# One filter's spectrum by dense products instead of two stages, fewer filler products, and a newly searched order

## The chip, the core and the metric

The kernel runs on one core of a Trainium2 chip. The core has a matrix engine (TensorE, "PE" in the profile, with its weight loads as "PEld"), a vector engine (DVE), an activation engine (ACT), a small general engine (POOL) and a queue engine (SP) that issues transfers to 16 DMA engines. Time is device microseconds for one launch, as a median of several runs. A profiled execution is a separate run with a trace; its span is counted from its first instruction to its last.

## What is computed

The input has one sequence of 2048 positions and 640 channels. Two layers follow each other, each with a residual:

```python
x = A_q
h  = x + q_ln * y            # q_ln = layernorm(x)
k_shift = short causal filter of k (4 taps per channel)
kv = k_shift * v
y  = causal convolution of kv with ssm_k (length 2048, per channel, by FFT) + kv * ssm_D
h2 = h + (silu(n @ w_gate) * (n @ w_up)) @ w_down     # n = layernorm(h), inner width 1728
```

## The kernel before

**Tiling.** The sequence is cut into 4 blocks (j = 0 to 3) of 512 positions, the channels into two column halves (c = 0, 1) of 320. For each block and half, the spectra of `kv` (called X) and of the filter `ssm_k` (called K) are formed on PE, multiplied with those of the earlier blocks on DVE, summed, and transformed back on PE. Then come the first residual (ACT and DVE), the layer norm (DVE, ACT, POOL), a transpose of the normalized block, and the feed-forward part: gate and up products into PSUM, SiLU on ACT, a product on DVE, and the down projection.

**Two ways to a spectrum.** `fwd` (line 659) and `spec` (line 741) do it in two stages. Stage one, named `s1`, is 4 groups of 2 matmuls (128x128 weights by 320 columns), each group evicted from PSUM by ACT (`e1`). Then four transfers within SBUF (`shK…`, `shX…`, 160 KB each) regroup the partitions. Stage two, named `s2`, is 4 groups of 4 matmuls with 128x64 weights, each group evicted by ACT (`e2`). `dense_h` (line 689) does it in one stage: 4 groups (`df`) of 8 matmuls of 128x128 weights by 320 columns, each group evicted by ACT or DVE (`de`), with no transfer between. Its tables (`DEN`, line 462) lie where the down-projection weights come later, so the loads `wd` wait for every dense group (line 701 collects them). Block 0 uses the dense way throughout. In block 1 the set `DFW` (line 351) names what goes the dense way: before, the filter K of the first half alone.

**Guard matmuls.** `warm` (line 542) makes matmuls of 512 columns on constants whose result nobody reads. `WARM` (line 339) asks for one run of 5 at the start and one run of 4; `FILL` (line 340) asks for four runs of 2. The order decides where they stand. In the order of before, the run of 5 and one run of 2 stand at the start, ahead of the first tap products, and the run of 4 and three runs of 2 stand among the work between the end of block 0's convolution and the start of its feed-forward part.

**The order.** No engine chooses at run time. A packed table (`_PLAN`, line 1327) holds, for each of the operations, its engine, its place in that engine's queue, its buffer, and some pacing of transfers; `plan` (line 101) unpacks it, and `emit` writes five instruction streams with the semaphore waits that the dependences need. Each engine runs its stream strictly in order. In the order of before, the two-stage spectrum of K of block 1's second half (`K11`) stands as follows on PE: three groups of `s1K11` together after the dense groups of `K10`, the fourth a little later between two guard runs, and the four groups of `s2K11` spread among block 0's gate and up products. On SP its four transfers `shK11` stand among the loads of the feed-forward weights; the last of them stands behind three weight loads.

Of the kernel before, what the change touches and what calls it, by code (L numbers as in the profile page):

```python
# [317 lines left out]
def bass_sequential_preLN__ssm_conv_h3__swiglu_ffn__prompt_kernel(  # L318
# [3 lines left out]
    _, S, D = A_q.shape  # L322
    F = B_w_gate.shape[1]
    assert (S, D, F) == (2048, 640, 1728)
    R = 4
    B = 128 * R
    NB = S // B
    N = 2 * B
# [10 lines left out]
    WARM = [5, 4]  # L339
    FILL = [2] * 4  # L340
# [10 lines left out]
    DFW = {("K",1,0)}  # L351
# [976 lines left out]
    "c-rlI2UJ^Ew)Q#dsGtfGl0XOv6%b7ziUdMPfT#k|d$GZkxWv78C+=~axc7n++i{C~Z*g3bICdP{vEv%Ixc8E{zKvoW%w*<eX3bkO|N3+9y1MtCv(Mh&{`PmSE{h`qA|it8z^<K$nl}O*xYg0J5fSN6?)ddiXm!;b"  # L1328
    "h49+{ZxPzY!LM5hZ!G`p-EY@_`}v=VNO+Si;jK}`*LKZqq(8m4-SF!?{(X19U6We%5?aOmN7w(l4q7wW`uIKT-)qyhPHo5jtM-I9iXi-r_5X(JzXk8_oMIQ>q`%Yp|EGHXQI$x4m-j#7|L^tvdp!MLDe=EO$3LT9"
    "!e8qBC!R6?{8Q#X|6KgP!rYp3((B`oTL1PNmhf-5ZmX=8NWVw?=UWJ_cQit)H<{*4n%~RFhytHPWPsKf6o+D6{S=o46WSTb4Qxn=ji`u+=!lD0NPsv<gOXj>bm;Lyo`{cxNDQqcmrp99!R`irny=|_#RN|r<PJV~"  # L1330
    "a7BZWTo@@v9?-@Fk3u9uQaA*#`yd(eMSe&EUOkW!`6Ct5x>`dasxOL1R_KjHMkGh!C=vWqz#rRX?FR7}fJg%VIbf><8wKDKp+FRZf{-3sgwU@;!6*zxfNwuIVjyo5GD8#v#EL@+$bxKO6N1uE28^<!RIpD$>3|>;"
    "<)AF&Km{ltvMWJls2s+|p=^|gicle7sX$fW&kTDIc=v#jdhpcDtp(Z=z;iZu$^Z{JfIc2oqZ(*UhTbHX4<~p@Lb+%l^jaad4fbTz4Mt_4cBliyu0$UInl#ji8UR^4^f7uDbw(Z0J8)l*=Acr*Pz_eaa5WlrMSW2("
    "u<eGLpnWzPf!;@>(0H^HbwWeY7&H#NZHLhl(1&OenvC|ME@%K6jE2G34d9ao%z6T&-cT<o)XNLlQ~+x-s7WYr+>Fu!84QA$Rgg;|_@F{n-Jt?J7^!fLlOZ*D@PR9DsEG>dpoU!w9ECx~xlqYy6a_Uch8)^M7IhH0"
    "8F?Mt)dKEZunGaIW;SafuXxyvz)mOB9q_)3dI08rfVl=L(jID(30!sqAM>DZKJ@fPi@|b%D-StD4uE)ih!_gmZ&pGyRIwR@70!WBdljfT0Ir%pW8kcXb1JZ&3AO8k`hx~CU{oX;0!;M;@59l1Xe6-O6A*QRDis3{"
    "<)9G<j2H@xmqBGC!P6*Ud<1Yl7JcO6yE`!71FBa9S{ev-`V>4Y0<Znha>#xuT7o`<_WtN|sKYwQuO7VBp_OR0EAmEA{1))n01+C|3b1YNnTHml+h`ipdNEv0K(o+A@Y{qogY9&%c>)#-p#Hl-IiI5!P~|nCfG;4{"
    "T13Dz!G1oP3##}CodGPnKoQfx>nret@sH>ybO~KSN<0sJhmN9S=mZkrS?DA>h0daL$QRE=U!iZ%A@l?C#B*S_MF78%z_Jn8)&U=7pxE}HluF378=3+fd<crU01;OK%9ZFj%xDAHCb?!tXQ+Jhd`W}(;sic(T*|jY"
    "Z!uK33Ro*~&7>^o%L3lZfuUMZL>*wB4m#-#*L^@qpP-q*?i92P;;aW&HUV4PAh#({kEu|N?qIVD7}^S4>_$7#m*{IW5h^+s>beKG=?rX)0=`D0{pc{-hYmoFM<CO0frVq}M|2uI&w-lF2KyoCI52Y%eGlB61zxUz"
    "{Wj!=Hz5lC5~@hU>k$c8x@L1D)PE|BoCs*gp&6i{k)Wl%fV&Ui9putl4`>+xeh0zc1N1xqDm4SNF%zAKY77J1^P!Flpe~nz^^@o-`WanA*U=4h6Wv1hAg5&ze>rGm1ma*R_Qnb<$NpG_HFzCVcr9q-4!R5ZZ3M6D"
    "fvbn;KGgC7dW;^SU(qk<8G4Fd!dJrqu-FfJ83Q~7U>Vk8KOBgoa43$&M?g{TcsJtW!@wT{Z%1^@!+g9Kxb(tI<bw|a;;#WY3$t-EryiJrM0h_`N`j|Dl!s7zgwH}2c6<jEd=C)(2>C?fUjYXhV|)(sO2ZWFhMAa-"
# [78 lines left out]
```

## Time and profile before

| | us |
|---|---|
| median of 3 runs | 278.29 (277.79 to 278.37) |
| the profiled execution's own time | 278.89 |
| its span, first to last instruction | 277.1 |
| PE busy in the span | 270.6 |
| DVE busy | 227.2 |
| ACT busy | 196.5 |

The span is 1.8 us under the profiled execution's own time, and that execution is 0.6 us over the median of the runs. A matmul's recorded duration contains its way through the array, so neighbouring records overlap: what one costs in a stream is the distance between the starts of neighbours, not its own duration, and "PE busy" hides waits of less than the overlap. In the timeline, a row gives its start, the time from its start to the end of its last instruction, the operation, the count, and in square brackets how long the engine was idle before it and what ended that.

### The profile page before, as it was taken

How to read it: one execution, taken by the hardware profiler on the slowest of the kernel's cores; microseconds unless marked ns; L12 is line 12 of the kernel's file. 1: busy time of each engine (PE TensorE's matmuls, PEld its weight loads, DVE VectorE, ACT ScalarE, POOL GpSimd, SP SyncE). 2: the span in 40 equal slices, each digit the busy share in tenths (PEclk: the TensorE clock that was granted, in tenths of full speed). 3: DMA queues.
4: the chain of work that ended last, by engine and by line, in shares of the span. 5: the costliest groups of instructions: out<-in, count | busy, mean ns of one | idle time of the engine just before them, and what ended most of it. 6: DMA issues, size and time to landing. Idle time of an engine off the chain costs nothing.

```text
span 277.1 us, 4869 instructions
## 1 busy us (share of the span) xinstructions
PE 270.6 (98%) x1761; PEld 149.6 (54%) x1761; DVE 227.2 (82%) x420; ACT 196.5 (71%) x319; POOL 13.7 (5%) x21
## 2 busy tenths in 40 slices
PE   8999999999999999999999999999999999999995
PEld 3677666454544476544444566444445766444573
DVE  3899999999999999999999999999997553015414
ACT  3479869999799988768998888879998740620000
POOL 1000200200000102000001002000001020000000
PEclk9999999999999999999999999999999999999999
DMA  6958969978978554775432664552021133000003
GB/s 189 288 161 269 242 183 261 280 225 255 334 232 251 178 158 120 140 261 145 150 99 73 169 174 128 167 195 84 22 75 54 51 62 106 12 0 0 0 14 107
DMA packets 54573, 40.97 MB, mean 148 GB/s; under 512 B 20243, under 2 KB 51732, under 8 KB 54550
## 3 DMA queue, kind: packets, MB, share of 16 engines
q1 hardware_dynamic: 54402, 40.63, 51.3%
q8 instruction: 14, 0.23, 0.3%
q14 instruction: 9, 0.07, 0.1%
q10 hardware_dynamic: 148, 0.04, 0.1%
HBM read 19.42 MB, written 2.62 MB: 80 GB/s over the span
## 4 chain that ended last, share of the span: by engine, by line
PE 74%; DVE 9%; DMA 8%; ACT 3%; SPq 2%; issue 1%; POOL 1%; ACTq 0%
PE ps L519 74%; DVE sb L751 9%; DMA sb<-sb 4%; DMA sb<-in_A_k_dram 3%; SPq L507 2%; ACT sb L921 1%; ACT sb L499 1%; POOL stt L878 1%; ACT sb L1097 1%; PE ps L1143 0%; DVE sb L1251 0%; DVE stt L877 0%; DVE stt L917 0%; SPq L227 0%; ACTq L227 0%
## 5 line engine op out<-in xcount | busy, mean ns | idle before, releaser
L519 PE MATMUL ps<-sb 128*128 128x320 bf16 (+3 forms) x1309 | 231.2, 332 | 2.3 <-DVE sb L533 1.1
L751 DVE TENSOR_TENSOR sb<-sb 128x1280 bf16<-128x1280 bf16 (+5 forms) x264 | 174.3, 722 | 1.8 <-ACT sb L499 1.0
L519 PEld LDWEIGHTS ps<-sb 128*128 128x128 bf16 (+2 forms) x1309 | 122.4, 98 | 96.7 <-issue 10.8
L499 ACT ACTIVATE sb<-ps 128x640 bf16<-128x640 f32 (+2 forms) x157 | 110.1, 758 | 24.5 <-PE ps L519 21.1
L519 PE MATMUL ps<-sb,tab 128*64 128x320 bf16 (+2 forms) x408 | 50.7, 302 | 1.3 <-DMA sb<-sb 0.6
L1198 ACT ACTIVATE sb<-ps 128x1024 bf16<-128x1024 f32 (+2 forms) x32 | 29.0, 919 | 19.3 <-PE ps L519 18.9
L519 PEld LDWEIGHTS ps<-sb,tab 128*64 128x64 f16 (+2 forms) x408 | 24.0, 101 | 25.6 <-issue 12.0
L751 DVE TENSOR_TENSOR sb<-ps,sb 128x1024 bf16<-128x1024 f32 (+3 forms) x18 | 15.8, 891 | 20.4 <-ACT sb L1198 15.4
L878 POOL TENSOR_TENSOR stt<-stt 128x2 f32<-128x2 f32 (+1 forms) x12 | 12.7, 1058 | 211.6 <-DVE stt L877 170.8
L1101 DVE SCALAR_TENSOR_TENSOR sb<-sb,stt 128x320 bf16<-128x320 bf16 x32 | 16.8, 544 | 5.6 <-ACT sb L1097 5.4
L1097 ACT ACTIVATE sb<-ps,stt 128x320 f32<-128x320 f32 x32 | 18.1, 620 | 4.2 <-PE ps L519 3.4
L921 ACT ACTIVATE sb<-sb,stt 128x640 uint8<-128x640 bf16 x16 | 13.3, 831 | 0.3 <-DVE stt L917 0.2
L1270 DVE SCALAR_TENSOR_TENSOR sb<-ps,stt,sb 128x640 bf16<-128x640 f32 x12 | 10.4, 879 | 2.8 <-PE ps L519 2.8
L1251 DVE SCALAR_TENSOR_TENSOR sb<-ps,stt,sb 128x320 bf16<-128x320 f32 x8 | 3.9, 546 | 10.4 <-PE ps L519 10.3
L914 ACT ACTIVATE sb<-sb 128x640 uint8<-128x640 bf16 x16 | 11.8, 737 | 0.2
L939 ACT ACTIVATE sb<-sb,stt 128x640 uint8<-128x640 bf16 x12 | 9.9, 827 | 0.9 <-DVE stt L934 0.7
L893 ACT ACTIVATE sb<-sb,stt 128x640 bf16<-128x640 bf16 x8 | 7.3, 920 | 1.7 <-DMA sb<-sb 1.0
L861 DVE BATCH_NORM_STATS2 stt<-sb 128x6 f32<-128x320 bf16 x8 | 3.8, 486 | 0.0
L892 DVE TENSOR_SCALAR sb<-sb,stt 128x640 bf16<-128x640 bf16 x8 | 3.4, 440 | 0.1
L500 DVE CAST sb<-ps 128x640 bf16<-128x640 f32 x1 | 0.8, 825 | 3.1 <-PE ps L519 3.1
L921 ACT ACTIVATION_READ_ACCUMULATOR sb<-sb,stt 128x1 f32 x16 | 3.2, 199 | 0.0
L646 PE MATMUL ps<-sb 128*128 128x128 bf16 (+1 forms) x24 | 3.2, 226 | 0.0
(24 smaller groups left out, 23.4 us busy)
## 6 DMA issues: line engine op xcount, KB each, us to landing
sb<-sb SPq DMA_DIRECT2D x68, 160.0 KB, 2.8
sb<-in_A_k_dram SPq DMA_DIRECT2D x6, 560.0 KB, 5.0
sb<-in_A_v_dram SPq DMA_DIRECT2D x8, 320.0 KB, 4.2
sb<-in_A_q_dram SPq DMA_DIRECT2D x8, 320.0 KB, 3.5
sb<-cst_den SPq DMA_DIRECT2D x8, 256.0 KB, 4.0
sb<-sb SPq DMA_DIRECT2D x24, 80.0 KB, 2.6
out_dram<-sb SPq DMA_DIRECT2D x12, 160.0 KB, 1.9
sb<-in_B_w_down_dram SPq DMA_DIRECT2D x3, 480.0 KB, 4.6
```

Source lines behind the costliest of these rows:

```text
L499: fns = {"act": lambda a: a.activation(out=dst(), in_=src(), func=ACTF.Copy), "dve": lambda v: v.tensor_copy(out=dst(), in_=src())}
L519: return lambda t: t.matmul(o(), l(), r(), start=st, stop=sp)
L751: return lambda v: v.tensor_tensor(out=o(), in0=a(), in1=b_(), op=op)
L878: P.op({"pool": 1.05}, lambda g: g.tensor_tensor(out=y, in0=va, in1=stt[:, oCO + 4:oCO + 4 + hi - lo], op=ALU.pow), c1 + [(ST, "half")], c ...
L893: "act": lambda a: a.activation(out=dst(), in_=src(), func=ACTF.Identity, scale=rs(l, j, b), bias=tmv(l, j, 3)[:, b:b + 1])},
L914: P.op({"act": act_c(D) + 0.22}, lambda a, b=b, jt=jt: a.activation(out=JU(jt), in_=V(xt, b * D, D), func=ACTF.Copy, accum_out=tmv(l, j, 4 ...
L921: P.op({"act": act_c(D) + 0.3}, lambda a, b=b, jt=jt: a.activation(out=JU(jt), in_=V(xt, b * D, D), func=ACTF.Square, bias=tmv(l, j, 5)[:, ...
L939: P.op({"act": act_c(D) + 0.3}, lambda a, b=b, jt=jt: a.activation(out=JU(jt), in_=V(xt, b * D, D), func=ACTF.Square, bias=tmv(l, j, 5)[:, ...
L1097: P.op({"act": act_c(CW, True)}, lambda a, k=k, b=b, wt=wt: a.activation(out=VF(wt, CW), in_=B32(pt, k, CW), func=ACTF.Identity, scale=tmv ...
L1101: vec(dve1(CW), lambda v, b=b, wt=wt, xv=xv: v.scalar_tensor_tensor(out=xv(), in0=xv(), scalar=tmv(0, j, 5)[:, b:b + 1], in1=VF(wt, CW), o ...
L1198: P.op({"act": act_c(n)}, lambda a: a.activation(out=dst(), in_=src(), func=ACTF.Silu), rd, wr, -1000, name=f"si{j}{i}")
L1270: vec(dve1(640), lambda v: v.scalar_tensor_tensor(out=hv(), in0=B32x2(pt, CW), scalar=tmv(0, j, 5)[:, b:b + 1], in1=hv(), op0=ALU.subtract ...
```

## The change

```diff
-    WARM = [5, 4]
-    FILL = [2] * 4
+    WARM = [5, 0]
+    FILL = [2] * 2
...
-    DFW = {("K",1,0)}
+    DFW = {("K",1,0),("K",1,1)}
...
 _PLAN = (
-    "c-rlI2UJ^Ew)Q#dsGtfGl0XOv6%b7ziUdMPfT#k|d$GZkxWv78C+=~axc7n++i{C~Z*g3bICdP{vEv%Ixc8E{zKvoW%w*<eX3bkO|N3+9y1MtCv(Mh&{`PmSE{h`qA|it8z^<K$nl}O*xYg0J5fSN6?)ddiXm!;b"
...
+    "c-rlI2Y8cJ-~KsCnxswI%qD5mCe3WR(lkv+R<oLPq)qoO-E;u5ktusBLqI_GP-Np^$ySg(<OO680Yw2t0Tmg__iJdO;_Lf=-|zFf{(jfzbFL>j&l$gQ-}gB@zzG2n5y5+7Zy}=Ai_muCwi`h^>EA54tq?lYTJ00s"
...
```

The filter spectrum of block 1's second half (`K11`) is made by `dense_h` too: `conv_c` (line 1109) then hands `spec` the transposed filter itself instead of the stage-one result, and `spec` calls `dense_h` for each of the four groups. The run of 4 guards and two of the four runs of 2 are gone. The rest is a new packed table: a new order for all engines, found by a search that varied orders twice as widely as before. The table is data of the planner, and its text does not show where an operation stands.

More of the change, by code (lines that the diff above doesn't have):

```diff
@@ L1382 @@
-    "l~o>I`mp+g@)4y6OIMXy+o@^-YBTEBG>mMVT{EZty@ve8H8r1h_@x84-n}8E!;-p-bxZ3FHHCHe8+45i8n4#gsSjwl*RZ>0bnUac!Ujd7qhVgdPYs(I(Z9IKvE;3L4Tb}$kT)EEZGUE42#l%W`~?bZ)p{5Wz#R$G"
-    "pl<*i)A3+JD&fC53n?7lZ|<7^GrjZ8T@(JR%71PD+h%X2?~a6Re`)5g?f;qW2%7Xpy$gs4QHa0y#Ss4D=dbPGy|w)%!9TKj`<DkT>-7k4-J>__`kU9oQD3irqq<s}uPCk-1fSH`?ag*%S8wx*JnHL}gBb3c*V8qx"
-    "lcT!M#5ZdKo5wZxVwX46>P&Xo{`SiW@*D3hs}G59&XhOENQmZYrM+I0M|-o1uNghjg_PE6B+-Q)yIKjZQRLT*{I(|VH<Uz|*XB0tibQi|Ky~4#xw53V#t>b3{Ju69xz_Vx*Lp#ctB34jitIx78=~f3%InN%u2`hk"
@@ new lines @@
+    "EI+l|(fae7&{oiY@bt9)`_KPB9tqFTB>ZL;v29#y8|mLJFJ8FK?w|Mcv`*^KOX%SDU)BHnI_QXG$NPEK&$)S#rx)k`cgJ^R2>-#@ze-%svBO?mNq^A#e^Vv@iY3w?;{MO@|D(P?$I|~qasQih?8qsp?fzT6|C2rD"
+    "Ki_5k-2Lyb6!UM@_5a=*pX-D0C)8h5R=a+l>*zmi!Oz}Vo_ZmAy%5{f=mRw(5+c3VGs!#B4_au54t*39fXIl6d=VS@qd>$#!N>$X{?N{ZIv?7CpfA#Ei427TWBs5`LR7Hf3xxtB8Hfvo4n1tJ5eW0xP^W?wA@qvi"
+    "*&jxSq7WoT60pmHqCiR%jv}B}j1o{Pd~1;tdW|Rp$&eY@VMc3w3?x82utf&@Jg9S^NMLptl7c55ibAnSjpAUA04!@z4AP+_uq{P$$l3t;q<|MWv{;Z8*^mQ8!<cmBhFO`&1GBSG4z#7AY?Oy`Q86ll{K`=>s)pNy"
@@ new lines @@
+    "3Q+;7KqcV63e|%>BiM_En0XLy0{C)3>?shh1x7o;OFCGw!?<Gbl@IMUuwexcx!^4uxuACp^gCgm3&v)k{@_0iHKJPRtwl4SB^~_K!RTr<6=KOp&8P{!8_;}+ssz=bN>qwEp^2yq>WyAPol$qR1R|V^hN9tUG<pqv"
+    "0zJdfDDX25eT-Vrc=RfojHaNyFuEW38;o8-tHCN2Sl|LHVSv2^a1H_lg<jmk0UH@)<b=rV=w*no0+6afZvZ3yFtT-C5R3@%G8zUpLg85mtf-(R0`S#9iAQA+Yb#3eC=vC9`CU*S)E8nH0`YZ%Y^tE-Lf)<X#lpze"
+    "yi_nh0hnun%xWR)ZjfIOGzeHI07NPwA`jT=iWZ_?=xrF)j21y&i@kb~!|Z6_AsoIVp(vmh1tk)!$H2D%*hm5fd%=u2;4TGN7yxJtL?ZybacCr(0AB0CYaQ@j1W}v4Y8nh)@_@ru1-**K0><M3(dp=QGz+3@f%v)r"
@@ new lines @@
+    "Go^r3AM_5evJ|ZLMJpiFRcJX{3HJM=_W|z>;Hv>x>WtQ)_W*^#Xd|qkZQ#8T_-aCPfW>7nXA0!>9oT*Ym|Xx&&q7~=GG?Q-z}qCq`X0=F7p(`IZ-M=X;BzTh*#slrMFcz*O+)iQE#pBy=fT4kv=ip7fo)+7BH?rB"
+    "68aonK?=MW9YROYG4v0_#jm3i=p;IYPNPsf2kin4?L)^AAJ2rf8|URu??p}n>!u8N=>%NV0ggQ&uGayJIp|A>bTP290{skYzjcNSv|9&Rl>#=!fM*5FEQGc!(0C@G>4xF~{>z{@6-oijr~-z&0vg?5-aN2c4v6*u"
+    "Kiwd+1(5rjko8+=9U!p@eSkKjt>AquAT$P0?}qlE9gyvZXg~T09fXWpSse*l+YShHhjFd^jz+s7w?pVKI*L9;2fPThW_}iMeG_cYgz<yX89?P6`V3tFM6RIgVE29GgEt^wydC^f@Oud3Mu@aGusI6wo&=VsgM!`!"
@@ new lines @@
+    "ZOjCX^aK9;fF1_H-52ya5Nbm}6|JkFE6iC4a~1)=m(WFMUjb~bgnX|7GhYDiH_%md3*AKDqHoam=q}{B3bI-W@sC1m9E{003`?*Qhhr^X4w_jEzQ01ZA>VbNg%3atchFDhGJ1f1K#$Om=rOvFenr2aCxFX(*b~-4"
+    "q+^i^%di|r;s_j#)i@3x1P#$4zW{syaHZib$PcqH2Y&*35MnwKVKJVCq<A*+#|*p^>;z&O65xHHfjyARcM!o(5bbHm$%4O!7`_7Co&z2X_y*+i0F-(Pa!kh*OvHZJ*E^;H{|wPlF%4e<T{plVQ@?<QG0eD$3Nan~"
+    "LkvHFrt0uoRFAosk3%8um+^XtM*{JO;{kXpL?OgdtiS{DCKLj3h5<VL@kUs$^|1B^!MYm&91I1XM#H*z4H%jLT)zYB<1Ao(8KvRd5dU3Zx(55hm?^;GY*>rCVAuQ*bn+2sYBMNjBOpD^yPIx+-aVkgt)Rs<uui9f"
@@ new lines @@
+    "3g-d;Ux0GH1P+sNJiZ1q&w$3v*n|^t6n0=6c40Tp0S3PToPPuxD<OjY;P)7c!LiW#8RUHu>2LzpV+}UqB%FfnI17{TEl}XMu-;by?!TaB{1`Q29)5&6<6lt|AWFqdcn-oL_%n$5C`5Y|J`aO-=YrlAfxa(-?k|Ai"
+    "FGK5jSRqS5Df3}n-GV3|L)4kr1Gc^boqUaoa0$-C`M3;s!d18$*MbrrfchRnw(o+bE`YW!AuCSB_dvCeAa5rwz!^9j=i*XajLUH)#Pbtk;QOH7)hGx*K`p>;7tk-pFJS`ij=SP+kQWj6!~v)`?gOieg5O6ya4*2e"
+    "2lvGc)DN=y09M^P6ana{K&ern)kquz`WXz^7_b$aL5;%z?F2yA0eTsVEndt_pqy7g*U5mS5eMKQuv!uUe<#E>0_y<XRL~a<4}x_)9H-+#h<O732xR~Yqe1;?kWUF711lm67vZsZ8{pH5$SC|FDh6D}!y0JiG8d1;"
@@ L1388 @@
+    "sLy|f%Zss)yu0Jmo%Tho{1K)dbA3_I|Em7a@b8G<^VkV(dk671IR6(cNS)I"
 )
```

98 lines of the change are left out of this document (42 added, 56 removed).

## The prediction

> **What bounds the kernel now.** I read the page's totals first, then the table by stretch, then the chain that ended last.
>
> ```profile
> span 277.1 us, 4869 instructions
> PE 270.6 (98%) x1761; PEld 149.6 (54%) x1761; DVE 227.2 (82%) x420; ACT 196.5 (71%) x319; POOL 13.7 (5%) x21
> ```
>
> ```profile
> core 0: us, PE busy (x) PEld busy (x) DVE busy (x) ACT busy (x) POOL busy (x), PEclk, DMA share, GB/s
> 44.00:55.00 11.00, 10.75 (x87) 5.97 (x84) 10.90 (x30) 10.79 (x18) 1.45 (x2) 1.00 1.04 280
> 55.00:80.00 25.00, 23.89 (x152) 12.40 (x149) 24.02 (x37) 23.39 (x37) 0.00 (x0) 1.00 0.89 269
> 80.00:212.00 132.00, 131.45 (x845) 66.81 (x844) 130.40 (x237) 115.16 (x189) 6.70 (x6) 1.00 0.49 141
> 212.00:231.00 19.00, 19.00 (x148) 12.98 (x145) 9.58 (x34) 10.20 (x20) 2.77 (x3) 1.00 0.30 77
> 231.00:274.20 43.20, 43.20 (x258) 24.20 (x255) 13.28 (x17) 7.23 (x8) 0.00 (x0) 1.00 0.07 23
> ```
>
> PE is busy to the end, so the time is a sum of PE's work and PE's waits. But the average hides a second limit: up to 212 us DVE is nearly full as well (it idles 0.1, 0.98 and 1.6 us in the first three stretches), and after 231 PE works alone. So a microsecond saved on PE before 212 counts only if the work that PE meets later is ready a microsecond earlier, and DVE makes that work. In 44 to 80, where the change sits, ACT is full too, and DMA.
>
> The chain that ended last (start, length, what) is mostly PE; one piece of it is not:
>
> ```profile
> 66.28 8.61 DMA sb<-sb
> ```
>
> At 66.28 the chain enters one transfer within SBUF that needs 8.61 us to land. By the kernel's order that is the last of the four `shK11`; its group of `s2K11` is the PE row at 74.92, shown below. Here the part that goes is itself on the chain.
>
> **The change part by part.** First, **what the dense groups add**: 32 matmuls of 128x128 by 320. Their price in a stream comes from rows of the same shape in block 0, from two windows of the timeline:
>
> ```profile
> 7.83 1.40 PE L519 MATMUL ps<-sb 128*128 128x320 bf16 x9
> ```
>
> ```profile
> 12.09 3.16 PE L519 MATMUL ps<-sb 128*128 128x320 bf16 x22 [0.50 <-DVE sb L751]
> ```
>
> Nine take 1.40 us and 22 take 3.16, each with one drain at its end, so a further one costs (3.16 - 1.40) / 13 = 0.135 us, and 32 cost +4.33 us.
>
> **What goes on PE.** The stretch between block 0's convolution and its feed-forward part:
>
> ```profile
> 47.66 2.10 PE L519 MATMUL ps<-sb,tab 128*128 128x320 bf16 x14
> 49.80 1.04 PE L519 MATMUL ps<-sb 128*128 128x512 bf16 x4
> 50.77 1.31 PE L519 MATMUL ps<-sb,tab 128*64 128x320 bf16 x10
> 51.92 0.59 PE L519 MATMUL ps<-sb 128*128 128x512 bf16 x2
> 52.44 0.46 PE L519 MATMUL ps<-sb,tab 128*64 128x320 bf16 x4
> 52.84 0.73 PE L1143 MATMUL ps<-sb 128*128 128x128 bf16 x10
> 53.41 1.03 PE L519 MATMUL ps<-sb 128*128 128x512 bf16 x4
> 54.42 0.72 PE L1143 MATMUL ps<-sb 128*128 128x128 bf16 x10
> ```
>
> The rows with 128x512 are the guards, 4 + 2 + 4 = 10. The two rows of line 1143 are the transposes of block 0's normalized rows. Stage one of `K11` is the first 6 matmuls of the first row and 2 in the third: 8 x 0.135 = -1.08 us. Four guards take 1.04 us and two 0.59, so one costs 0.45 / 2 = 0.225 us. I take it that one of the two remaining runs of 2 stays at the start and one here, so 8 go: -1.80 us.
>
> Stage two of `K11` stands in three places later, 4, 8 of 12, and 4 matmuls:
>
> ```profile
> 63.74 0.46 PE L519 MATMUL ps<-sb,tab 128*64 128x320 bf16 x4 [0.47 <-ACT sb L1198]
> 64.13 1.25 PE L519 MATMUL ps<-sb 128*128 128x512 bf16 x5
> ...
> 66.75 1.06 PE L519 MATMUL ps<-sb,tab 128*64 128x320 bf16 x12
> 67.74 1.80 PE L519 MATMUL ps<-sb 128*128 128x512 bf16 x10
> ...
> 73.82 0.46 PE L519 MATMUL ps<-sb,tab 128*64 128x320 bf16 x4
> 74.92 0.46 PE L519 MATMUL ps<-sb,tab 128*64 128x320 bf16 x4 [0.64 <-DMA sb<-sb]
> 75.32 1.47 PE L519 MATMUL ps<-sb 128*128 128x512 bf16 x6
> ```
>
> From start to next start: 0.39, 2/3 of 0.99 = 0.66, and 0.40, together -1.45 us, the cost of changing the array's shape included. Work on PE therefore changes by 4.33 - 1.08 - 1.80 - 1.45 = **0.0 us**: the dense way costs about what the guards and the two stages cost.
>
> **Waits that go.** At 74.92 PE waited 0.64 us for the transfer, and the records hide a little more (73.82 to 74.92 is 1.10 us for 0.40 us of work, so 0.70). Without it the next thing on PE is the gate and up product at 75.32, whose operands other rows already use. -0.70 us. In the stretch from 47.66 to 49.80, 6 x 0.135 and two stage-two groups at 0.40 account for 1.61 of 2.14 us; the other 0.5 us are waits for PSUM and evictions. A dense group is one long run between two evictions, and could cover them: between 0 and -0.5 us, and I take -0.3, since ACT, which evicts both, is full there. Sum on PE: 0.0 - 0.7 - 0.3 = **-1.0 us**.
>
> **ACT and the transfers.** Four `e1` and four `e2` evictions become four `de`; four transfers of 160 KB go.
>
> ```profile
> L499 ACT ACTIVATE sb<-ps 128x640 bf16<-128x640 f32 x135 | 88.6, 707 | 19.0 <-PE ps L519 18.4 <-DMA sb<-sb 0.2
> ```
>
> ```profile
> sb<-sb SPq DMA_DIRECT2D x68, 160.0 KB, 2.8
> ```
>
> ```profile
> 64.67 0.46 SPq L507 DMA_DIRECT2D sb<-in_B_w_down_dram  x1
> ```
>
> That is 4 x 0.71 = 2.8 us less on ACT, which has 1.6 us of idle time between 55 and 80, and 0.64 MB, at 269 GB/s 2.4 us of DMA time, taken out of the stretch that loads the feed-forward weights. I count it at nothing by itself: it is what lets the PE waits above go without a new one. The down-projection weights now wait for the dense groups of `K11`, which hold their place; if these stand at 47 to 56 us nothing is late, because the first such load issued only at 64.67 (last row).
>
> **What DVE gets.** The late transfer passed on along the engines:
>
> ```profile
> 75.43 1.30 ACT L499 ACTIVATE sb<-ps 128x640 bf16<-128x640 f32 x2 [1.41 <-PE ps L519]
> 76.17 1.63 DVE L751 TENSOR_TENSOR sb<-sb 128x640 bf16<-128x640 bf16 x3 [0.31 <-ACT sb L499]
> ```
>
> So of DVE's 0.98 us of idle time in 55 to 80 at least 0.31 go, and all at best. What of the 1.0 us reaches the end is decided at two gates. One is at 116.83 us:
>
> ```profile
> 116.83 1.24 PE L519 MATMUL ps<-sb 128*128 128x512 bf16 x5 [0.37 <-DMA sb<-sb]
> ```
>
> PE has run out of other work and waits for block 1's transposed rows. If it comes 1.0 us earlier, it waits longer, unless block 1's norm is earlier. DVE's sum up to there is fixed, but what it does in which order is not: products of block 2 stand between those of block 1, and with `K11` ready some 20 us sooner the products of block 1 can move ahead. The other gate is the last block:
>
> ```profile
> 228.35 1.20 SPq L1135 DMA_TRANSPOSE sb<-sb  x1
> ```
>
> ```profile
> 231.97 0.59 PE L519 MATMUL ps<-sb 128*128 128x512 bf16 x2
> ```
>
> ```profile
> DMA to landing us min/median/max: 2.6/2.6/2.6
> ```
>
> The last transposed rows land at 228.35 + 2.6 = 230.95 and are used at 231.97, so PE may be 1.02 us earlier there without any help from DVE. Gates that give 0.31 to 0.98 us (DVE) plus up to 1.02 us pass most of 1.0; I take off 0.2 for the first, where DVE alone decides: **-0.8 us**. The span goes from 277.1 to 276.3, the profiled execution from 278.9 to 278.1, and the median, 0.6 us under the profiled execution, from 278.3 to 277.5.
>
> **A rule that speaks against it.** The first guards, in two windows of the timeline:
>
> ```profile
> 1.05 2.31 PE L519 MATMUL ps<-sb 128*128 128x512 bf16 x5 [1.05 <-DVE sb L533]
> ```
>
> ```profile
> 2.74 3.45 PE L519 MATMUL ps<-sb 128*128 128x512 bf16 x10
> ```
>
> Five guards start between 1.05 and 2.74, 0.42 us apart, against 0.225 at 49.80: PE starts at half its rate. From 7.83 on (above) it is at full rate. The Trainium skill (TensorE: Matmul & The Clock Gate, Part 1) says that the array's clock is halved until it has been busy for about 3.4 us, and again after an idle window. The rows agree on the start; by that rule removing guards could bring the half clock back. In 44 to 55 the dense groups keep PE busier than the guards did, so there it does not apply.
>
> **The rivals.** (a) *The gain is given back.* The first gate does not move: DVE is as full as before, the new order has other waits of the size of those that went (0.3 to 0.7 us each), and PE comes early only to wait. For it speaks that DVE's 130.40 of 132 us leave no room; against it the 1.02 us at the last gate. Result: 0 to -0.5, say 278.1. (b) *Slower: the dense run delays DVE.* Place: 47.66 to 55.1. The transposes at 52.84 and 54.42 came as soon as block 0's norm was there, so the guards cost nothing there. Into those 7.5 us (to 54.42 + 0.72) now go 4.33 us for 1.08 + 1.80 + up to 0.5: it overflows by about 1.0 us. If the transposes and the stage-two groups of X and `K10` stand behind it in PE's queue, DVE's products start 1 us later:
>
> ```profile
> 54.12 10.71 DVE L751 TENSOR_TENSOR sb<-sb 128x1280 bf16<-128x1280 bf16 x14
> ```
>
> They run for 10.71 us without a pause, so DVE cannot regain it: 278.3 + 1.0 = 279.3. It decides once DVE's idle time in 44 to 80 rises from 1.1 to over 2 us. (c) *The clock.* If neither run of 2 stays at the start, PE idles 2 x 0.42 us there, and full rate may come later by that much or, at most, by as long as the half rate can have lasted, 1.05 to 7.83. A delay t costs t / 2 of work, and the wait of 0.50 us at 12.09 absorbs as much: 0.84 us cost nothing, 6.8 us cost 3.4 - 0.5 = 2.9, the middle 1.4: 277.5 + 1.4 = 278.9. (d) *The new order does more than the change.* PE's waits named above and shape changes elsewhere are open to a better order; twice the forecast, 276.6 or less.
>
> **How the numbers follow.** Forecast 0.45 (own range 276.8 to 277.7), (a) 0.27, (b) 0.18, (c) 0.04, (d) 0.06. The range leaves out half of (b), half of (c) and half of (d), 0.14: 276.3 to 279.2. A measurement of this kernel tells about 0.2% (0.56 us) from no change. Forecast and (d) lie beyond it, so faster 0.51; (a) within it, 0.27; (b) and (c), 0.22.
>
> **What would show it.** Right: a run of 32 matmuls of 320 columns between 45 and 56 us; no transfer within SBUF in the chain near 66 to 75; no wait of PE for `sb<-sb` before 100 us; ACT's evictions of 640 columns down from 135 to 131 (or fewer, if DVE takes some); PE's wait at the first gate no longer than 0.5 us. Wrong: DVE idle over 2 us in 44 to 80 (b), a longer wait at about 116 (a), or 320-column products 0.27 us apart after 6 us (c). What would overturn the whole sum is a new order that moves waits of over a microsecond in blocks 1 to 3, which nothing in the profile of before can show.

## The result, and the profile after

The change makes the kernel slower by a little. Its median is 279.79 us over 8 runs (278.74 to 280.33), beside 278.01 us for the kernel before on the same chip (8 runs, 277.17 to 278.40): ratio 1.0059, 95% interval 1.0044 to 1.0073. The forecast was 277.5 us, with 276.3 to 279.2 as its range. Two single runs further below, of 281.94 and 282.29 us, fell in a slower state of the chip and are left out of the ratios.

The profiled execution took 279.77 us, with a span of 277.9 (before: 277.1). The page's totals:

```profile
span 277.9 us, 4848 instructions
PE 270.8 (97%) x1761; PEld 151.9 (55%) x1761; DVE 227.3 (82%) x418; ACT 196.3 (71%) x317; POOL 14.5 (5%) x21
PEclk9799999999999999999999999999999999999999
```

PE's busy time is within 0.2 us of before, but this execution holds a stretch at half rate, shown below, that adds about 1.4 us to it. Two executions of the kernel after without such a stretch have 267.8 and 267.5 us, beside 268.9 us in a second execution of the kernel before. The 7 in the second slice of the clock is new. The same stretches as before (columns: PE, PEld, DVE, ACT, POOL busy, then the granted clock, DMA share, GB/s):

```profile
44.00:55.00 11.00, 11.00 (x92) 7.34 (x90) 10.90 (x32) 10.29 (x17) 1.71 (x2) 1.00 0.94 281
55.00:80.00 25.00, 24.39 (x161) 13.50 (x159) 25.00 (x38) 23.91 (x38) 0.00 (x0) 1.00 0.82 235
80.00:212.00 132.00, 130.86 (x839) 66.92 (x837) 129.54 (x236) 113.09 (x185) 7.98 (x7) 1.00 0.49 142
```

From 55 to 80 DVE has no idle time left (0.98 us before). But from 80 to 212 it now idles 2.46 us, 0.9 more. Where the dense groups went, in the timeline of PE:

```profile
50.82 1.25 PE L519 MATMUL ps<-sb 128*128 128x320 bf16 x8
52.00 0.46 PE L519 MATMUL ps<-sb,tab 128*64 128x320 bf16 x4
52.39 2.35 PE L519 MATMUL ps<-sb 128*128 128x320 bf16 x16
54.58 0.72 PE L1143 MATMUL ps<-sb 128*128 128x128 bf16 x10
55.13 1.68 PE L519 MATMUL ps<-sb 128*128 128x512 bf16 x10
```

The rows of 8 and 16 are three of the four groups; the fourth is 8 of the 10 matmuls of the row at 55.13, whose other two are a guard run of 2 (the row is named by its first shape). The other remaining run of 2 stands at 32.3 us. So none stays at the start, where 5 guards of 7 are left.

The start, in the timeline of PE and, with the clock, in windows of 1 us:

```profile
5.78 1.60 PE L646 MATMUL ps<-sb 128*128 128x128 bf16 x12
8.13 4.02 PE L519 MATMUL ps<-sb 128*128 128x320 bf16 x16 [0.76 <-DVE sb L751]
```

```profile
8.00:9.00 1.00, 0.86 (x4) 0.56 (x5) 1.00 (x2) 1.00 (x2) 0.00 (x0) 0.62 0.91 291
9.00:10.00 1.00, 1.00 (x6) 0.53 (x4) 1.00 (x2) 0.24 (x1) 0.00 (x0) 0.50 0.28 86
10.00:11.00 1.00, 1.00 (x6) 0.52 (x5) 1.00 (x2) 0.00 (x0) 0.00 (x0) 0.50 0.90 224
11.00:12.00 1.00, 1.00 (x7) 0.64 (x6) 0.10 (x1) 0.00 (x0) 0.00 (x0) 0.67 0.78 219
```

The clock is at half for (0.38 + 0.5 + 0.5 + 0.33) / 0.5 = 3.4 us, and 16 matmuls need 4.02 us. Late in the kernel stands a wait that before did not have. In the chain that ended last, and in the timelines of PE and DVE:

```profile
174.72 2.60 DMA sb<-sb
177.32 0.09 issue
177.41 3.81 PE ps L519 x19
181.22 0.02 issue
181.25 1.31 ACT sb L499 x2
182.55 0.02 issue
182.58 12.61 DVE sb L751 x21
```

```profile
177.41 3.40 PE L519 MATMUL ps<-sb 128*128 128x512 bf16 x15 [0.96 <-DMA sb<-sb]
```

```profile
182.58 4.24 DVE L751 TENSOR_TENSOR sb<-sb 128x1280 bf16<-128x1280 bf16 x7 [0.86 <-ACT sb L499]
```

PE waits for the transposed rows of block 2, and 0.86 us of that wait reaches DVE. The timeline of SP tells why the last transpose is issued so late:

```profile
174.03 0.59 SPq L507 DMA_DIRECT2D sb<-sb  x1
174.72 1.26 SPq L1135 DMA_TRANSPOSE sb<-sb  x1
176.03 0.58 SPq L507 DMA_DIRECT2D out_dram<-sb  x1
176.72 3.78 SPq L507 DMA_DIRECT2D sb<-sb  x6
180.55 0.58 SPq L507 DMA_DIRECT2D out_dram<-sb  x1
181.23 0.52 SPq L507 DMA_DIRECT2D sb<-sb  x1
183.03 0.35 SPq L507 DMA_DIRECT2D sb<-in_A_q_dram  x1
```

In the new order a store (`st13`) and a shuffle (a transfer within SBUF, `shX30`) stand between block 2's four transposes. Before, the four were issued back to back from 168.5 on. Rows of that timeline of SP, the first with the last of them:

```profile
173.14 1.20 SPq L1135 DMA_TRANSPOSE sb<-sb  x1
...
175.62 1.57 SPq L507 DMA_DIRECT2D out_dram<-sb  x3
...
184.20 0.58 SPq L507 DMA_DIRECT2D sb<-in_A_q_dram  x1
```

Two more rows of the kernel after matter below: the store at 180.55 (`st10`) and the load at 183.03 (`x30`), which needs the place in SBUF that the store empties. Before, `st10` is among the three stores at 175.62, and `x30` is the load at 184.20.

### The profile page after: what moved, and what is told of

It is laid out like the page before. It is cut to its first block, busy times and chain, and to the rows that moved or that the text cites. A ratio compares the mean times of both kernels' runs of the same rounds, so it can differ in the third digit from the quotient of the medians.

```text
span 277.9 us, 4848 instructions
## 1 busy us (share of the span) xinstructions
PE 270.8 (97%) x1761; PEld 151.9 (55%) x1761; DVE 227.3 (82%) x418; ACT 196.3 (71%) x317; POOL 14.5 (5%) x21
## 4 chain that ended last, share of the span: by engine, by line
PE 81%; DVE 10%; DMA 4%; ACT 2%; issue 1%; SPq 0%; ACTq 0%
PE ps L519 80%; DVE sb L751 10%; DMA sb<-in_A_v_dram 2%; DMA sb<-in_A_k_dram 2%; ACT sb L499 1%; DMA sb<-sb 1%; PE ps L646 1%; ACT L1198 0%; PE ps L1143 0%; SPq L507 0%; ACT sb L1198 0%; ACT sb L914 0%; DVE sb L1251 0%; DVE stt L917 0%; ACTq L227 0%
## 5 line engine op out<-in xcount | busy, mean ns | idle before, releaser
L519 PE MATMUL ps<-sb 128*128 128x320 bf16 (+2 forms) x1333 | 234.8, 332 | 3.8 <-DVE sb L533 1.4
L519 PEld LDWEIGHTS ps<-sb 128*128 128x128 bf16 (+1 forms) x1333 | 125.8, 98 | 99.2 <-issue 12.5
L499 ACT ACTIVATE sb<-ps 128x640 bf16<-128x640 f32 (+2 forms) x152 | 108.2, 758 | 29.0 <-PE ps L519 22.3
L519 PE MATMUL ps<-sb,tab 128*64 128x320 bf16 (+2 forms) x384 | 47.0, 302 | 0.2
L519 PEld LDWEIGHTS ps<-sb,tab 128*64 128x64 f16 (+2 forms) x384 | 22.9, 101 | 21.8 <-issue 9.4
L878 POOL TENSOR_TENSOR stt<-stt 128x2 f32<-128x2 f32 (+1 forms) x12 | 13.5, 1130 | 211.2 <-DVE stt L877 183.5
L893 ACT ACTIVATE sb<-sb,stt 128x640 bf16<-128x640 bf16 x11 | 10.2, 923 | 2.0 <-DVE stt L885 1.3
L500 DVE CAST sb<-ps 128x640 bf16<-128x640 f32 x2 | 1.6, 820 | 2.6 <-PE ps L519 2.6
L914 ACT ACTIVATION_READ_ACCUMULATOR sb<-sb 128x1 f32 x16 | 3.2, 201 | 0.0
```

What stands on the lines that cost most here:

```text
L499: fns = {"act": lambda a: a.activation(out=dst(), in_=src(), func=ACTF.Copy), "dve": lambda v: v.tensor_copy(out=dst(), in_=src())}
L519: return lambda t: t.matmul(o(), l(), r(), start=st, stop=sp)
L878: P.op({"pool": 1.05}, lambda g: g.tensor_tensor(out=y, in0=va, in1=stt[:, oCO + 4:oCO + 4 + hi - lo], op=ALU.pow), c1 + [(ST, "half")], c ...
L893: "act": lambda a: a.activation(out=dst(), in_=src(), func=ACTF.Identity, scale=rs(l, j, b), bias=tmv(l, j, 3)[:, b:b + 1])},
L914: P.op({"act": act_c(D) + 0.22}, lambda a, b=b, jt=jt: a.activation(out=JU(jt), in_=V(xt, b * D, D), func=ACTF.Copy, accum_out=tmv(l, j, 4 ...
```

## The experiments

Each kernel is compared with the kernel before on its own chip. The median of the kernel after moves by 1 us between two sets of its runs, as the first experiment shows, and its ratio with it (1.0059 and 1.0031); the median of the kernel before stays between 277.6 and 278.0 us in all the sets compared. So the ratios are what to read, and two kernels whose intervals overlap are not told apart. In the expectations `kvp00` is the row of 16 matmuls behind the first transposes, `m2o100` a product on DVE near 66 us and `gm21` one near 187 us.

**The start.** The kernel after, unaltered, once more:

> The changed kernel, unaltered. Both theories: ratio 1.004 to 1.007 against the kernel before. Theory S (the start): the trace shows a stretch of half clock after the first grant, between 5 and 15 us, in which the products of kvp00 are 0.27 us apart, or a first grant later than 6.5 us. Theory O (the order): whatever the clock does at the start, DVE idles 2 us or more between 80 and 212, over the 1.6 us of before.

278.81 us (277.06 to 280.02, 12 runs), ratio 1.0031 (1.0013 to 1.0049). The profiled execution was its fastest, with full rate behind the first transposes:

```profile
7.67 2.61 PE L519 MATMUL ps<-sb 128*128 128x320 bf16 x16
```

These are the same 16 matmuls that took 4.02 us above. So the half rate comes in some executions, and costs PE 1.4 us where it comes. How often is not known: of the 20 timed runs of the kernel after in these two sets, five have a mean granted clock of 0.993 or 0.994, as 3.4 us at half in 278 us give, but a full rate that comes late leaves no such mark (see the last section). The five are not the slowest five. Then two guards more at the start of the kernel after:

```diff
-    WARM = [5, 0]
+    WARM = [7, 0]
```

> The changed kernel with 7 instead of 5 guards at the start, as many as the kernel before has there. Theory S: no half clock after the first grant, the dense groups of block 0 start about 1 us sooner, ratio 0.999 to 1.002. Theory O: the start does not reach the end; ratio stays at 1.004 to 1.008, or 0.4 us more because the tap products start 0.85 us later.

279.32 us (278.44 to 280.08, 6 runs), ratio 1.0056 (1.0035 to 1.0077): no half rate in the profile, and no gain. Theory S alone does not hold, although the two guards also cost something: DVE's first eviction comes at 5.14 us in place of 4.29. Four guards ahead of the first transposes of the filter instead:

```diff
+            if (j, c) == (0, 0):
+                fns = [mm(lambda: B32(pt, 0, 512), lambda: V(ONE, 0, 128), grhs, True, True)] * 4 + fns
```

> The changed kernel with 4 more guards right ahead of block 0's first filter transposes, so that they fill the 0.76 us in which PE waited before kvp00, without delaying the tap products. Theory S: the clock stays granted, kvp00 takes 1.1 us per run instead of 2, ratio 0.998 to 1.002. Theory O: 1.004 to 1.007.

278.44 us (277.17 to 280.40, 12 runs), ratio 1.0021 (1.0001 to 1.0041): no half rate in the profile, and an interval that overlaps that of the kernel after unaltered. And the kernel before with two guards fewer at its start:

```diff
-    WARM = [5, 4]
+    WARM = [3, 4]
```

> The kernel before with 3 instead of 5 guards in its first run, so 5 at the start in all, as the changed kernel has. Theory S: the start now loses the clock here too in some or all executions, ratio 1.002 to 1.006. Theory O: ratio 0.999 to 1.001.

279.60 us (277.63 to 280.65, 9 runs), ratio 1.0049 (1.0021 to 1.0078), in two groups: three runs at 277.6 to 277.8, six at 279.2 to 280.6. The profile is one of the second group, with the 16 matmuls at half rate:

```profile
8.56 4.09 PE L519 MATMUL ps<-sb 128*128 128x320 bf16 x16
```

So taking two guards from the start is enough to put most runs of the kernel before outside its narrow band, and theory O alone does not hold either. Last, both kernels with a start made slow and alike (13 fills of SBUF on DVE ahead of the first tap eviction, 34 guards ahead of the first transposes of the filter):

> The changed kernel with a longer start that is the same whatever the clock's phase: 13 memsets (about 8 us) on DVE ahead of its first tap eviction, and 34 guards on PE ahead of the first filter transposes. All transfers of the start have landed by then and the clock is granted. About 8 to 9 us slower than the kernel before in any case; what counts is the difference to t2. Theory S (the loss is at the start): 0.2 to 0.8 us below t2. Theory O (the loss is in the order behind the start): 0.8 us or more above t2.

> The kernel before with the same longer start. Theory S: above t1 by 0.2 to 0.8 us. Theory O: below t1 by 0.8 us or more. Both: all executions within 1 us, because the clock's phase no longer matters.

296.15 us (295.15 to 297.55, 6 runs) after, 296.50 us (295.77 to 297.13, 4 runs) before. The equal start was meant to be free of the half clock, and was not: in both profiles PE waits 8.48 us for the fills ahead of its guards, and runs at half rate for a stretch behind that. The two come out alike within their spread. With few runs, that says only that no loss of over a microsecond is left where the start is the same.

**Parts of the change in the old order.** The dense groups at the places of stage one, with the rest of the old order kept and eight guards of the middle out:

> The kernel before in its own order, with the change's parts alone: the dense groups of K11 at the places of its stage one, stage two and the four transfers out, the run of 4 guards and two runs of 2 out (the start keeps its 7). If the dense way pays as the prediction's sum says: ratio 0.996 to 0.999. If the wait at 74.92 was an accident of one execution: 0.999 to 1.001. If the dense run delays DVE (the prediction's rival b): 1.002 or more, with DVE's products of block 1 later by the same.

279.75 us (279.37 to 280.29, 6 runs), ratio 1.0075 (1.0058 to 1.0093). The timeline of DVE shows where:

```profile
56.17 0.45 DVE L892 TENSOR_SCALAR sb<-sb,stt 128x640 bf16<-128x640 bf16 x1 [2.64 <-PE ps L1143]
```

The dense run stands ahead of block 0's transposes on PE, and DVE waits for them: rival (b), of 2.6 us rather than 1.0. The searched order of the kernel after avoids it: there one of the four groups stands behind the first of these transposes, and DVE has no idle time from 55 to 80. Then these eight guards out of the old order and nothing else (the second expectation counts six; it is eight):

> The kernel before in its own order without the run of 4 and two runs of 2 among the guards before block 0's feed-forward part; the start keeps its 7, K11 keeps its two stages. If those guards only fill a wait: ratio 0.999 to 1.001. If they cost PE time: 0.995 to 0.998 (1.8 us at most). If the clock needed them: half rate after 49 us and 1.002 or more.

> The kernel before without six of its guards in the middle (the order and the start of the kernel before). Its timed runs lay between 277.5 and 280.6 us, its one profiled execution at 278.2 us with no half-rate matmul behind the start and idle time of DVE of 0.4 us from block 0's layer norm to 90 us. If the clock is lost where the guards were, near 55 us, a slow execution shows matmuls at half rate there; if not, a slow execution shows its time in DVE's waits for transfers, with TensorE at full rate throughout.

278.87 us (277.46 to 280.55, 12 runs), ratio 1.0041 (1.0021 to 1.0061). Both profiled executions (278.19 and 278.02 us) show no half rate behind the start, and in neither is a transfer within SBUF on the chain near 66 us: that wait went without the dense way, and the kernel became slower, not faster. What puts half of its runs above 279 us stays open, as no profile fell on one of them.

**Further executions of both.**

> The kernel before once more, for a look at a second execution of it. If its first profiled execution was untypical, this one has a span of 275.5 to 276.3 us, and the wait of DVE for the shifted columns at 76 to 78.5 us (0.67 us in the profile of before) is not there; DVE's idle time from 55 to 80 us is then below 0.6 us in place of 0.98. If it was typical, span 277 us and the same two waits.

> The kernel after once more, for a look at a third execution. Whatever the start does here, the time from the first half of block 3's last layer norm on DVE to the end is 57.7 us (57.5 in the kernel before), DVE waits about 0.4 to 0.9 us at 180 to 183 us and 0.2 to 0.8 us near 66 us. If the full clock is kept at the start, the span is 275.5 to 277; if it is lost for a stretch of 3.4 us, 277 to 278.5 us, with the first dense group of block 0 some 1.5 us later.

> The kernel after once more. In three executions so far the time from the start to the first layer norm of block 0 held idle time of DVE of 1.8, 0.3 and 1.6 us, and matmuls at half rate between 7.8 and 11.5 us in the first and the third, none in the second. If the start decides: a span of 277 us or more goes with half-rate matmuls behind 7.8 us, one below 276.5 us without. If the waits behind 60 us decide, the span goes with DVE's wait at m2o100 (0.0 to 1.2 us) in place of that.

The kernel before: 278.01 us, span 276.2, with the same chain piece at its place, and PE waits 0.64 us behind it again, so the wait that was to go is a regular one (on SP six weight loads, not three, stand between this transfer and the transfer of `K11` ahead of it):

```profile
65.56 8.61 DMA sb<-sb
```

The kernel after: 279.29 us (span 277.5) with the 16 matmuls in 3.78 us from 7.79, and 277.82 us (span 276.0) without half rate. Up to 212 us DVE is nearly full, so a wait of DVE should stay in the time to the end. That makes a ledger of the profiled executions possible: the gaps between DVE's instructions in each trace, summed by stretch (us; "start" is the time of DVE's first product of the short filter, "rest" what is left of the span, DVE's work included). The rest is nearly the same in all six, which bears this out.

| | start, and gaps to block 0's norm | gaps from there to 90 us | 90 to 176 | behind block 2's transposes | rest to the end | span |
|---|---|---|---|---|---|---|
| before, profiled | 7.17 | 1.08 | 1.59 | 0 | 267.2 | 277.1 |
| before, second | 6.50 | 1.09 | 1.44 | 0 | 267.2 | 276.2 |
| after, profiled (half rate) | 8.36 | 0.45 | 1.17 | 0.86 | 267.1 | 277.9 |
| after, second | 6.38 | 0.40 | 1.11 | 0.42 | 266.9 | 275.3 |
| after, third (half rate) | 7.38 | 1.33 | 0.99 | 0.83 | 266.9 | 277.5 |
| after, fourth | 6.25 | 1.25 | 1.03 | 0.82 | 266.7 | 276.0 |

The new order gains 0.2 us (mean) before 90 us, 0.4 from 90 to 176 and 0.3 in the rest: 0.9 us. It gives back 0.7 us behind block 2's transposes, and 1.0 to 2.1 us at the start in the half-rate executions, against the others. In the column to 90 us the 1.33 and 1.25 are a wait for other transfers within SBUF, the four that lay out block 2's filter (`shk20`): the place into which DVE's product goes is the one that they read from. In the timeline of DVE of the fourth execution:

```profile
66.27 2.30 DVE L751 TENSOR_TENSOR sb<-sb 128x1280 bf16<-128x1280 bf16 x3 [1.11 <-DMA sb<-sb]
```

**The order, one transfer at a time.** These change only the order on SP, given as lists. First block 2's transposes together:

```diff
- tr23 tr22 st13 tr20 shX30 tr21
+ tr23 tr22 tr20 tr21 st13 shX30
```

> The kernel after with one thing changed: on SP the four transposes of block 2 are issued back to back (tr23, tr22, tr20, tr21), ahead of the store st13 and of the shuffle into shX30 that stand between them in the order of the kernel after. Theory 'order' (part of the loss is the wait that this order makes): the wait of PE for block 2's transposes at about 177 us (1.0 us in the profile after) falls below 0.3 us, DVE's wait at about 181 us (0.4 to 0.9 us) falls below 0.3 us, and the median goes 0.4 to 0.8 us below the 278.8 us of the kernel after unaltered: 278.0 to 278.4 us. Theory 'start' (the whole loss is in the first 12 us): the first wait may go, yet the next one takes its place, and the median stays within 0.2 us of 278.8 us. A third way: the shuffle into shX30, now later, is missed in its turn, and a wait for sb<-sb of the same length stands behind 181 us.

277.91 us (276.53 to 281.94, 12 runs; three above 279), ratio 1.0000 (0.9977 to 1.0023), the outcome that theory 'order' gave. PE's wait fell from 0.96 to 0.27 us and DVE's behind it is gone. The profiled execution (279.38 us) shows a new one, in the chain that ended last and in DVE's timeline:

```profile
179.01 4.39 DMA out_dram<-sb
...
183.49 2.96 DMA sb<-in_A_q_dram
186.45 0.02 issue
186.47 0.83 ACT sb L914 x2
187.30 0.92 ACT sb L1198
188.22 0.02 issue
```

```profile
188.24 2.16 DVE L751 TENSOR_TENSOR sb<-sb 128x1024 bf16<-128x1024 bf16 x3 [2.32 <-ACT sb L1198]
```

The store `st10` needs 4.39 us to land. SP, which runs in order, then issues `x30` into its place; ACT's row sums of `x30` stand ahead of the SiLU that DVE wants. Before, some 8 us lay between the two, so that a slow store cost nothing. The same with the four guards of the third experiment:

> The kernel before this one in the list with four guard matmuls of 512 columns ahead of the first transposes of k as well, so that TensorE has more work in the window in which the kernel after sometimes loses its full clock. If 'start' and 'order' each hold a part of the loss, the two add: below the guards alone (278.4 us) by 0.4 to 0.8 us, that is 277.6 to 278.0 us, within 0.2 us of the kernel before or ahead of it. If only 'start' counts: 278.3 to 278.5 us as with the guards alone. If only 'order' counts: as the transposes alone. In the profile no stretch of half-rate matmuls behind the first transposes.

277.78 us (277.07 to 279.97, 12 runs), ratio 1.0002 (0.9982 to 1.0022). That is within the range for two parts that add, but no lower than with the transposes alone, so these runs do not show that the guards add anything. Then `shk20` too:

```diff
- shk20 shk20 wu23 shk20 wd shk20
+ shk20 shk20 shk20 shk20 wu23 wd
```

> The kernel with block 2's transposes issued together and four guards ahead of the first transposes of k, and one thing more: on SP the four transfers that shift block 2's rows of k (shk20, 80 KB each) stand together, ahead of a 320 KB load of w_up and one of w_down that stood between them. Theory 'a new wait in place of the old': DVE's wait at m2o100 near 66 us (0.0 to 1.3 us in seven executions of the new order, on average 0.7) falls below 0.2 us, and the median falls by 0.4 to 0.8 us from 277.8: 277.0 to 277.4 us, ahead of the kernel before by about 0.5 us. Rival: the two loads are missed in their turn, or another wait takes its place, and the median stays within 0.2 us of 277.8. A cost is bounded by the 1.2 us by which the two weight loads are issued later.

279.25 us (277.19 to 282.29, 12 runs), ratio 1.0021 (0.9996 to 1.0046). The wait at 66 us is gone, and the 11 runs that count fall into two groups, four at 277.2 to 277.6 and seven from 278.7 to 280.4. The profile (279.24 us) is of the second, and has the wait behind the store again (from the added guards on, lines are numbered 5 higher):

```profile
188.09 2.16 DVE L756 TENSOR_TENSOR sb<-sb 128x1024 bf16<-128x1024 bf16 x3 [1.83 <-ACT sb L1203]
```

The source of `st10` is ready at 173.8 us, when DVE has ended the addition that makes it, so it can go much sooner. In this kernel, and in the one before it:

```diff
- st12 shK31 shX30 shX31 shX31 shK31 shK31 st10 shX31 x30
+ st12 st10 shK31 shX30 shX31 shX31 shK31 shK31 shX31 x30
```

> The kernel of f3_shuffles_first_too with one store moved: st10 (164 KB, its data ready at 173.8 us, issued at 179.3 because SP has six shuffles ahead of it) is issued right behind st12, near 175.5 us. The load of x30 needs the place that st10 empties; where st10 took 3.9 us to land, x30 was issued at 183.3, ACT's row sums of x30 came at 186.3, and DVE waited 1.8 us at gm21 behind them. Theory 'store': this makes the upper of the two groups of times of that kernel (277.2 to 277.6 us in four runs, 278.7 to 280.4 in seven); with the store earlier no wait at gm21, all or nearly all runs at 277.2 to 277.8, median about 277.4 us, ahead of the kernel before (277.9). Rival: the two groups have another cause (the clock at the start); then the median stays near 279 us and the spread at 3 us.

> The kernel of f2_transposes_first_guards_start with the store st10 moved in the same way, and the shifted rows shk20 left where they were. Theory 'store': the runs of f2 above 278.1 us go (5 of 12), median 277.4 to 277.7 us. Against f4_store_earlier it tells what the wait at m2o100 (about 0.7 to 1.3 us in the profiles) is worth: if that is a loss of its own, f5 is 0.5 to 1 us above f4; if it is made up for by DVE's later waits, within 0.2 us.

With `shk20` together: 277.68 us (277.09 to 278.56, 12 runs), ratio 0.9997 (0.9986 to 1.0009). Without: 277.41 us (276.75 to 278.25, 12 runs), ratio 0.9981 (0.9970 to 0.9993), the one kernel here that is ahead of the kernel before. In both no run is above 279, of 24; without the move of the store there were six of 11 and one of 12. SP of the first of them now issues the load much sooner, and DVE runs from 173.72 on without a pause:

```profile
174.28 1.09 SPq L507 DMA_DIRECT2D out_dram<-sb  x2
175.47 4.41 SPq L507 DMA_DIRECT2D sb<-sb  x7
180.06 0.46 SPq L507 DMA_DIRECT2D sb<-in_A_q_dram  x1
```

```profile
173.72 16.65 DVE L756 TENSOR_TENSOR sb<-sb 128x1280 bf16<-128x1280 bf16 x27
```

The wait at 66 us is 1.2 us in the profile of the faster kernel, which fell on the slowest of its 12 runs, and 0 in that of the other. So taking it away is worth nothing that these runs can tell, against what the ledger would say; why not, and whether the faster runs have the wait, they do not show. Last, the store alone moved in the kernel after:

> The kernel after with one change alone: the store st10 issued right behind st12, four positions of shuffles earlier on SP; start, guards and transposes as in the kernel after. Theory 'store' (the largest part of the loss is the late landing of st10, which in some executions holds x30, ACT and then DVE at 187 us): 277.7 to 278.2 us, and the runs above 279 us go but for those with half-rate matmuls at the start. Theory 'start' (the store counted only once the start was mended): 278.6 us or more, spread as in the kernel after (277.1 to 280.0). Theory 'gate' (the wait for block 2's transposes at 177 us is a loss of its own of 0.4 to 0.9 us beside the store): 278.2 to 278.6 us.

278.36 us (276.96 to 280.02, 12 runs), ratio 1.0028 (1.0011 to 1.0044): two of 12 runs are above 279 (of the 22 of the kernel after, 10), but the ratio is not told from the 1.0031 of the kernel after unaltered. Of the three edits, each by itself, only the transposes issued together bring the median level with the kernel before, and none brings it ahead.

## Why the prediction was wrong

**Right: the price of the dense groups, and the transfer that goes.** The 16 matmuls at 52.39 take 2.19 us to the start of the next row, 0.137 us each beside a forecast 0.135. No transfer within SBUF is left in the chain near 66 to 75, and PE has no wait for one before 100 us. Whether the sum of 0.0 us of work holds is not shown: without half rate PE's busy time is 1.1 to 1.4 us below before, and it holds hidden waits as well as work. ACT's evictions of 640 columns fell from 135 to 130:

```profile
L499 ACT ACTIVATE sb<-ps 128x640 bf16<-128x640 f32 x130 | 86.8, 706 | 18.1 <-PE ps L519 17.3
```

DVE lost its idle time from 55 to 80 in the profiled execution. The first gate held no wait: block 1's feed-forward part began at 117.04 with none shown.

**Mis-sized: what the waits are worth.** The forecast put -0.7 us on the wait at 74.92. The wait is regular, and it went. But in all four executions of the kernel after PE waits 0.61 us for a SiLU of ACT near 65 us (before it waited 0.47 us for one at 63.74); in the profiled execution the chain that ended last goes through this wait, behind a load of ACT's table of 1.28 us. The row of the second execution:

```profile
64.61 2.66 PE L519 MATMUL ps<-sb 128*128 128x512 bf16 x13 [0.61 <-ACT sb L1198]
```

And on DVE a wait for `shk20` at 66 us, 0 to 1.2 us, came in place of the old ones (means of the gaps to 90 us over the executions: 1.09 us before, 0.86 after). That is rival (a), at places it did not name. The gain of 0.9 us that the ledger shows comes mostly from 90 us on.

**The step that failed first: "What of the 1.0 us reaches the end is decided at two gates".** I took the gates of the old order, at 116.83 and in the last block, for all of them, and took off 0.2 us. In the new order a third decides, block 2's transposes at 177.41: 0.4 to 0.9 us on DVE, and issuing them together brought the ratio of the kernel after to 1.0000. A fourth is the store `st10` behind it. That its late landing costs up to 2.3 us is shown in two kernels with the transposes first, and in one of them moving it took the upper group of times away (six of 11 above 279 us, then none of 12). In the kernel after itself no profile caught it, and moving it alone there changed nothing that the ratios can tell. The prediction's last sentence allowed for such a wait and gave it no chance of its own.

**The second: "I take it that one of the two remaining runs of 2 stays at the start and one here".** None stayed. Rival (c) hung on that, and had 0.04. Of the profiled executions with five guards at the start and none added ahead of the first transposes of the filter, 3 of 7 show a half-rate stretch behind 7 us (the kernel after in 2 of 4, the kernel before with two guards fewer in its one); of the 11 with seven guards, or with the four added, none, the slow-start pair left aside. Its price of 1.4 us came out, in part by luck, since it was the middle of 0 to 2.9 us. In two of the three the full rate came late, as I had priced it (its first record stands at 10.7 and 12.1 us); in the profiled execution of after it came in time and then fell for 3.4 us, which I had not thought of.

**Against the rule.** The Trainium skill (TensorE: Matmul & The Clock Gate, Part 1) has the clock halved after an idle window of about 3.4 us, and the prediction used it to dismiss a loss in 44 to 55; there it holds, at 1.00 in all profiles. So it does in the slow start of the kernel after, where the clock falls at 9.1 us, within PE's wait of 8.48 us. At the start of the kernel after itself the trace agrees with the length, 3.4 us at half, and differs on the cause: between the grant and the fall PE's longest wait is 0.76 us, between 12 short transposes and the products. What these transposes count for is not tested. The same part says that the window in which the activity is counted runs free, so that executions of one kernel differ in when the full rate comes; the four profiles of the kernel after agree (first on record at 4.1, 4.8, 7.2 and 10.7 us).

**What remains.** The kernel after is slower by 0.9 to 1.6 us (ratios of its two sets of runs). Start, transposes and store mended together take it to 0.5 us below the kernel before (277.41 beside 277.9). That this is near the forecast's -0.8 does not confirm the forecast, which was for another order. How the loss divides among the three is not settled: alone they take the ratio from 1.0031 and 1.0059 to 1.0021 (start), 1.0000 (transposes) and 1.0028 (store), and these intervals overlap. Nor do the runs part the dense way from the new order: in the old order it cost 0.75%, in the new one with the three mended it stands in a kernel 0.2% ahead.

## What to carry to other kernels

In a kernel with a fixed order, a new order is a change of its own: look in every in-order queue for loads that reuse a place just emptied by a store, and for transfers that a gate needs, and ask how much slack each had before and has now. Removing filler work at the start can move a full clock that only just held; look at several executions, since one profile shows one of the ways it can go. If a change widens the spread of the runs, look for a wait that comes only sometimes, and remove its cause, before judging the change by its median.

## Unexpected of the hardware

The clock fell back to half for 3.4 us after it had been granted, with no wait of PE over 0.76 us between the grant and the fall. Where the full rate came late, the clock column does not show it. The window from 9 to 10 us in the third execution of the kernel after, and then in the kernel before:

```profile
9.00:10.00 1.00, 1.00 (x6) 0.55 (x4) 1.00 (x2) 0.73 (x2) 0.00 (x0) 1.00 0.80 239
```

```profile
9.00:10.00 1.00, 1.00 (x9) 0.73 (x8) 1.00 (x1) 0.77 (x2) 0.00 (x0) 1.00 0.74 247
```

Both say 1.00, with 6 matmuls in the microsecond and with 9. So the spacing of equal matmuls is the safer sign. And the landing of block 1's stores, 160 KB each, took 1.9 to 4.4 us in the executions of the new order (1.9 to 2.5 in those of the old), which was enough to make the times of one kernel fall into two groups.
